# Attention and squared-ReLU FFN on one core: the last TensorE transposes of the steady loop go to DMA, the attention half behind them moves earlier, and one load moves behind a transpose

## The chip, the cores and the metric

The kernel runs on one core of one Trainium2 chip. The metric is device time in microseconds (us), the median of several executions. Only one execution of each run has a trace.

The engines are named as in the traces: TensorE (PE) does the matrix products, VectorE (DVE), ScalarE (ACT) and GpSimd (POOL) the element-wise work, and SyncE (SP) issues the transfers (DMA). PSUM is the on-chip memory that the products of this kernel are written to, in buffers called banks; SBUF is the on-chip memory of all its other tiles.

## The reference

```python
# q, k, v: (8, 8, 576, 64) float32; w_in: (512, 2048); w_out: (2048, 512)
scores = (q @ k.T) / sqrt(64)                      # per batch and head
mask = (rel >= 0) & (rel < 64)                     # causal window of 64
attn = softmax(where(mask, scores, -1e9)) @ v
x = attn.transpose(0, 2, 1, 3).reshape(4608, 512)
h = maximum(x @ w_in, 0)
out = (h * h) @ w_out                              # (4608, 512)
```

The 4608 tokens are nine blocks of 512. A block has four attention tiles of 128 tokens, two pairs.

## The kernel before

After a start of some 74 us, which brings the weights and works on the first blocks, the kernel is a loop of stages. A stage weaves four things by a position between 0 and 1: the down-projection of block g-1 (seven products in place of eight, in 14 steps), the up-projection of block g (16 groups of four matmuls), the attention of block g+1 and the loads for later ones. The events are sorted by position; that order is the program order of every engine.

```python
def attention(g):
    c = 4 * g
    ev = []
    dx = 0.34 if g == 3 else 0.275
    def sc(i):
        S_(i); expo(i)                     # TensorE scores, ScalarE exponential
        later(2, lambda: keep(i))          # VectorE mask, two ticks later
        tick()
    def to_xT(i):
        if g == 3:
            X(i)                           # four TensorE transposes
            copy_xT(i)                     # VectorE, out of PSUM
            tick()
        else:
            if i % 2:
                dma_xT(i // 2)             # one DMA transpose for a pair
    def va(i):
        V(i); norm(i); tick()              # TensorE values, VectorE normalisation
    for h in range(2):
        a, b, t = c + 2 * h, c + 2 * h + 1, 0.46 * h + (0.1 if g == 3 else 0.0)
        ev += [(t + 0.02, lambda a=a: sc(a)), (t + 0.021, lambda b=b: sc(b)),
               (t + 0.25, lambda a=a: va(a)), (t + 0.251, lambda b=b: va(b)),
               (t + dx, lambda a=a: to_xT(a)), (t + dx + 0.0001, lambda b=b: to_xT(b))]
    return ev

def UP(g, f):                              # one up-projection group
    hps = ps_up.tile([P, 512], FP32, name="hps", tag="ps_u")     # two buffers in PSUM
    ...                                    # four matmuls
    hrelu = hrp.tile(...)
    nc.scalar.activation(out=hrelu[:], in_=hps[:], func=AF.Relu)
    if f in SQ_ACT or g == 2 and f in (2, 9):
        ...                                # square on ScalarE, from hrelu
    else:                                  # square on VectorE, from hps and hrelu
        nc.vector.scalar_tensor_tensor(out=h2_of(g)[:, f, :], in0=hps[:], scalar=0.0,
                                       in1=hrelu[:], op0=ALU.max, op1=ALU.mult)
    tick()

def loads(p):
    for h in range(2):
        t, a = 0.46 * h, p + h
        ...                                # (t + 0.06) DMA transposes of k and q of pair a
            ev.append((t + (0.28 if a - 1 == TAILS[1] else 0.14), lambda a=a, x=kq: load(a + 1, x)))
            ev.append((t + 0.3, lambda a=a, x=kq: load(a + 1, "kqv"[len(x):])))
```

A load also carries the work that GpSimd does with it: casts to half precision and, for values, copies between two buffers. `S_` of tile i writes a PSUM bank that the normalisation of two tiles before has to free. SyncE issues all transfers in program order, so one that waits holds all behind it (run e7 below has the cost of such a place). `TAILS` names two pairs, 10 and 15, whose loads are arranged differently; `tick()` counts steps of the program, and `later(2, ...)` puts work two steps further down.

The softmax here doesn't subtract the row's maximum and nothing guards it: scores larger than these inputs give would overflow.

Of the kernel before, what the change touches and what calls it, by code (L numbers as in the profile page):

```python
# [40 lines left out]
def kernel(  # L41
# [16 lines left out]
    TAILS = (10, 15)  # L58
# [27 lines left out]
    def later(n, fn):  # L86
        if n == 0:
            fn()
        else:
            put_off.append([n, fn])  # L90

    def tick():
        for e in list(put_off):
            e[0] -= 1
            if e[0] <= 0:
                put_off.remove(e)
                e[1]()
# [65 lines left out]
    def fetch_tail(nm, p):  # L163

        src = {"k": k, "q": q, "v": v}[nm]
        for i in (2 * p, 2 * p + 1):
            if nm == "q":
                if i % 2 == 0:
                    st = two_tiles()
                sts[nm, i] = st[:, i % 2]  # L170
                for n in range(2):
                    fetch_rows(sts[nm, i], src, tail_seq(i) + n, S - 64, 64, 64 * n)
            else:
                st = sts[nm, i] = two_tiles()
                for n in range(2):
                    fetch_rows(st[:, n], src, tail_seq(i) + n, S - 128)
# [92 lines left out]
    def copy(eng, out, in_, scale=1.0):  # L269
        if eng is nc.scalar:  # L270
            nc.scalar.activation(out=out, in_=in_, func=AF.Copy, scale=scale)  # L271
        elif scale == 1.0:
            eng.tensor_copy(out=out, in_=in_)  # L273
        else:
            eng.tensor_scalar(out=out, in0=in_, scalar1=scale, scalar2=None, op0=ALU.mult)
# [19 lines left out]
    def cast_q(i, eng=nc.gpsimd):  # L295
        copy(eng, pair16(q16s, "q16", i // 2)[:, i % 2], sts["q", i])

    def cast_v(i, eng=nc.gpsimd):
        copy(eng, v_evs[i % NV][:, :, 0:D], sts["v", i])
# [15 lines left out]
    def xT_of(g):  # L315
        if g not in xTs:
            xTs[g] = xtp.tile([P, 4, DMC, P], FP16, name="xT", tag="xT")
        return xTs[g]
# [37 lines left out]
    def att_bank(name, dtype=FP32):  # L356
        return ps_att.tile([P, 2, 512], FP32, name=name, tag="ps_a")
# [59 lines left out]
    def S_(i):  # L417
        sc = att_bank("sc")
        scv = sc[:].rearrange("p a (h b t) -> p a h b t", h=HP, b=2)
        for a in range(2 if i < 4 else 0):  # L420
            nc.tensor.matmul(sc[:, a, :], ident[:], minus[i > 0], start=True, stop=False,
                             skip_group_check=True)
        for hp in range(HP):
            for blk in range(2):
                for hh in range(2):
                    r0 = 64 * hh
                    qT = q_cols(i)[r0:r0 + 64, hp, :]
                    qT = qT[:, 64 * blk:64 * blk + 64]
                    nc.tensor.matmul(scv[:, hh, hp, blk, :], keys(i, hp, r0, blk), qT,  # L429
                                     start=i >= 4, stop=True, skip_group_check=i < 4)  # L430
        scs[i] = sc
        pms[i] = attw.tile([P, 2, HP * 2 * 64], FP16, name="pm", tag="pm")

    def expo(i, part=slice(0, 2)):
        nc.scalar.activation(out=pms[i][:, part], in_=scs[i][:, part], func=AF.Exp,  # L435
                             scale=1.0 / float(D) ** 0.5)

    def keep(i, part=slice(0, 2)):
        mask = mask_first if is_first(i) else mask_inner
        nc.vector.tensor_tensor(  # L440
            out=pms[i][:, part], in0=pms[i][:, part],
            in1=mask[:].rearrange("p (o a) r -> p o (a r)", o=1)
            .to_broadcast([P, part.stop - part.start, 512]), op=ALU.min)

    def V(i):
        ps = att_bank("av")
        avs[i] = ps[:, :, 0:4 * 66].rearrange("p a (h e) -> p a h e", h=4)
        for h in range(H):
            for blk in range(2):
                vv = (v_ods if blk == 0 else v_evs)[i % NV]  # L450
                h0 = h // 2 * P + blk * 64
                nc.tensor.matmul(  # L452
                    avs[i][64 * blk:64 * blk + 64, h // 4, h % 4, 0:65],
                    pms[i][:, h % 2, h0:h0 + 64], vv[:, h, 0:65], start=True, stop=True)

    def norm(i):
        if i // 2 not in xs:
            xs[i // 2] = attw.tile([P, 2, 2, HP, D], FP16, name="x_sb", tag="x_sb", bufs=2)
        rden = smallp.tile([P, 2, 4, 1], FP32, name="rden", tag="rden")
        nc.vector.reciprocal(out=rden[:], in_=avs[i][:, :, :, 64:65])  # L460
        nc.vector.tensor_tensor(  # L461
            out=xs[i // 2][:, i % 2], in0=avs[i][:, :, :, 0:D],
            in1=rden[:].to_broadcast([P, 2, 4, D]), op=ALU.mult)

    def xT_cols(i):
        return xT_of(i // 4)[:, i % 4]

    def X(i):
        xps[i] = att_bank("xt_ps")[:, 0, :].bitcast(FP16)[:, 0:DMC * P].rearrange(
            "p (c t) -> p c t", c=DMC)  # L470
        for c in range(DMC):
            nc.tensor.transpose(out=xps[i][:, c, :],  # L472
                                in_=xs[i // 2][:, i % 2, c // 2, 2 * (c % 2):2 * (c % 2) + 2, :],
                                identity=ident[:])

    def copy_xT(i, eng=nc.vector):
        copy(eng, xT_cols(i), xps[i])

    def dma_xT(p):

        nc.sync.dma_start_transpose(
            out=xT_of(p // 2)[:, p % 2 * 2:p % 2 * 2 + 2].rearrange("p n c t -> p (n c) t"),
            in_=xs[p][:].rearrange("p n a h d -> p (n a h d)"))
# [234 lines left out]
    def attention(g):  # L718
        c = 4 * g
        ev = []  # L720
        dx = 0.34 if g == 3 else 0.275

        def sc(i):
            S_(i)
            expo(i)
            later(2, lambda: keep(i))
            tick()

        def to_xT(i):
            if g == 3:  # L730
                X(i)
                copy_xT(i)
                tick()
            else:
                if i % 2:
                    dma_xT(i // 2)

        def va(i):
            V(i)
            norm(i)  # L740
            tick()

        for h in range(2):
            a, b, t = c + 2 * h, c + 2 * h + 1, 0.46 * h + (0.1 if g == 3 else 0.0)
            ev += [(t + 0.02, lambda a=a: sc(a)), (t + 0.021, lambda b=b: sc(b)),
                   (t + 0.25, lambda a=a: va(a)), (t + 0.251, lambda b=b: va(b)),
                   (t + dx, lambda a=a: to_xT(a)), (t + dx + 0.0001, lambda b=b: to_xT(b))]
        return ev

    def load(p, part):  # L750

        if p in TAILS:
            for nm in part:
                fetch_tail(nm, p)
        else:
            for nm in part:
                fetch_two(nm, p)
        both = (2 * p, 2 * p + 1)
        if "k" in part:
            for i in both:  # L760
                if p in TAILS:
                    k16s["tail", i] = st16.tile([P, 2, H, D], FP16, name="k16", tag="k16")
                    nc.gpsimd.tensor_copy(out=k16s["tail", i][:], in_=sts["k", i][:])
                else:
                    cast_k(i)
        if "q" in part:
            for i in both:
                cast_q(i)
        if "v" in part:
            for i in both:  # L770
                if p in TAILS:
                    for n, vv in enumerate((v_ods, v_evs)):
                        nc.gpsimd.tensor_copy(out=vv[i % NV][:, :, 0:D], in_=sts["v", i][:, n])
                else:
                    cast_v(i)
                    shift_v(i)
# [6 lines that stand above are left out]
            if a < NCK // 2:  # L783
                ev.append((t + 0.06, lambda a=a: (dma_k(a), dma_q(a))))
                if a not in TAILS:
                    ev.append((t + 0.3, lambda a=a: halo_apart(a)))
            if a + 1 < NCK // 2:
                kq = "k" if a + 1 in TAILS else "kq"
                ev.append((t + (0.28 if a - 1 == TAILS[1] else 0.14), lambda a=a, x=kq: load(a + 1, x)))
                ev.append((t + 0.3, lambda a=a, x=kq: load(a + 1, "kqv"[len(x):])))  # L790
        return ev

# [3 lines left out]
    for g in range(2, NTB + 1):  # L796
# [3 lines left out]
        ev = even(out_seven(g - 1))  # L800
# [39 lines left out]
```

## Time and profile before

| | before |
|---|---|
| median of 3 (later of 6) | 293.33 us (292.78) |
| span of the profiled execution | 290.4 us |
| beginning of the loop (first down-projection group) | 74.19 us |
| that group to the next stage's: edited stage, then the two after it | 30.44, 28.92, 28.88 us |
| TensorE waits after 74 us, with a releaser | one, 0.2 us |

A stage between two such beginnings has 28.9 us of matmuls. The edited stage is longer by 1.5: 0.9 are transposes, and 0.57 are a score group, because its first half sits 0.1 later than elsewhere and the next stage's does not. So TensorE has no slack after 74 us: work taken from it should shorten the kernel.

### The profile page before, as it was taken

What the parts mean: (1) busy time and instruction counts of PE and PEld (TensorE: products, weight loads), DVE (VectorE), ACT (ScalarE), POOL (GpSimd) and SP (SyncE); (2) the same over time, 40 slices, a digit from 0 to 9 for tenths busy, and PEclk for the clock granted to TensorE, in tenths of its full rate; (3) what the DMA queues carried; (4) which work ended last, traced back from release to release, by engine and by line L of the source; (5) the groups of instructions that cost most, each with busy time, mean ns of one, the idle gap of its engine ahead of it and who ended that gap; (6) DMA issues with size and microseconds to landing.
All of it is one profiled execution on the core that took longest, in us unless ns stands there. A gap on an engine that the chain in (4) does not pass through costs nothing.

```text
span 290.4 us, 7514 instructions
## 1 busy us (share of the span) xinstructions
PE 284.5 (98%) x3062; PEld 197.3 (68%) x3062; DVE 212.6 (73%) x393; ACT 192.2 (66%) x304; POOL 114.7 (40%) x171
## 2 busy tenths in 40 slices
PE   7999999999999999999999999999999999999995
PEld 5768888755666766666666666666666666666684
DVE  3779998869967776766887687668767876554493
ACT  2789898959777576757575857485748575666500
POOL 3702967757337702525564735250537300000000
PEclk9999999999999999999999999999999999999999
DMA  7999999989999678999999989699969802300143
GB/s 216 342 392 302 287 288 297 367 217 233 168 218 178 142 211 183 219 184 279 202 223 216 275 191 213 136 279 213 250 112 278 150 2 64 119 0 2 72 109 109
DMA packets 151842, 57.64 MB, mean 198 GB/s; under 512 B 128256, under 2 KB 143616, under 8 KB 151808
## 3 DMA queue, kind: packets, MB, share of 16 engines
q1 hardware_dynamic: 151808, 57.16, 82.4%
q8 instruction: 24, 0.39, 0.6%
q14 instruction: 10, 0.08, 0.1%
HBM read 38.80 MB, written 9.44 MB: 166 GB/s over the span
## 4 chain that ended last, share of the span: by engine, by line
PE 88%; DVE 6%; ACT 2%; DMA 2%; SPq 2%; issue 0%; POOL 0%; POOLq 0%
PE hps L530 32%; PE opsC L616 10%; PE opsD L616 9%; PE hps L502 8%; PE opsA L616 8%; PE ops L576 5%; PE opsB L616 5%; PE av L452 4%; PE sc L429 3%; DMA v_st<-in_v_dram 2%; DVE hs_all L604 1%; PE xt_ps L472 1%; DVE pm L440 1%; SPq L130 1%; DVE x_sb L461 1%; ACT pm L435 1%
## 5 line engine op out<-in xcount | busy, mean ns | idle before, releaser
L530 PE MATMUL hps<-xT,w_in_sb 128*128 128x512 f16 x448 | 112.9, 379 | 0.2 <-DVE h L540 0.2
L534 ACT ACTIVATE hrelu<-hps 128x512 f32<-128x512 f32 x112 | 66.7, 597 | 63.7 <-PE hps L530 63.4
L616 PEld LDWEIGHTS <-h 128*128 128x128 f16 x624 | 60.5, 98 | 20.7 <-issue 0.2
L530 PEld LDWEIGHTS <-w_in_sb 128*128 128x128 f16 x448 | 42.4, 98 | 32.7 <-issue 0.4
L540 DVE SCALAR_TENSOR_TENSOR h<-hps,hrelu 128x512 f16<-128x512 f32 x54 | 37.2, 689 | 32.3 <-ACT hrelu L534 32.1
L273 POOL COPY v_od<-v_ev 64x512 f16<-64x512 f16 x54 | 38.2, 707 | 6.3 <-ACT v_ev L271 2.4
L537 ACT ACTIVATE h<-hrelu 128x512 f16<-128x512 f32 x58 | 36.5, 630 | 1.6
L435 ACT ACTIVATE pm<-sc 128x1024 f16<-128x1024 f32 (+1 forms) x40 | 35.4, 941 | 3.3 <-PE sc L429 3.3
L616 PE MATMUL opsA<-w_out_sb,h 128*128 128x256 f16 x240 | 31.0, 273 | 0.0
L616 PE MATMUL opsD<-wb_all,h 128*128 128x256 f16 x240 | 30.9, 273 | 0.0
L616 PEld LDWEIGHTS <-hs_all 128*128 128x128 f16 x256 | 25.0, 98 | 8.6
L502 PE MATMUL hps<-xT,w_in_sb 128*128 128x256 f16 x256 | 30.1, 273 | 0.0
L502 PEld LDWEIGHTS <-w_in_sb 128*128 128x128 f16 x256 | 24.2, 98 | 3.0
L273 POOL CAST k<-kq_st 128x512 f16<-128x512 f32 x17 | 11.9, 697 | 35.6 <-DMA kq_st<-in_k_dram 35.6
L461 DVE TENSOR_TENSOR x_sb<-av,rden 128x512 f16<-128x512 f32 x36 | 24.9, 692 | 1.2
L440 DVE TENSOR_TENSOR pm<-pm,mask_inner 128x1024 f16<-128x1024 f16 x25 | 20.2, 811 | 5.8 <-ACT pm L435 5.8
L273 POOL CAST q<-kq_st 128x512 f16<-128x512 f32 x22 | 14.5, 658 | 14.9 <-DMA kq_st<-in_q_dram 14.4
L638 DVE SCALAR_TENSOR_TENSOR osb_all<-opsD,u 128x512 f32<-128x512 f32 x14 | 9.7, 691 | 11.3 <-PE opsD L616 11.3
L273 POOL CAST v_ev<-kq_st 128x512 f16<-128x512 f32 x16 | 12.5, 778 | 11.3 <-DMA kq_st<-in_v_dram 10.8
L616 PE MATMUL opsC<-w_out_sb,h 128*128 128x256 f16 x128 | 16.4, 273 | 0.0
L616 PE MATMUL opsC<-w_out_sb,hs_all 128*128 128x256 f16 x128 | 16.4, 273 | 0.0
L616 PE MATMUL opsB<-wb_all,hs_all 128*128 128x256 f16 x128 | 16.4, 273 | 0.0
(104 smaller groups left out, 374.1 us busy)
## 6 DMA issues: line engine op xcount, KB each, us to landing
kq_st<-in_k_dram SPq DMA_DIRECT2D x26, 256.0 KB, 3.9
kq_st<-in_v_dram SPq DMA_DIRECT2D x24, 256.0 KB, 4.1
out_dram<-osb_all SPq DMA_DIRECT2D x12, 512.0 KB, 4.1
kq_st<-in_q_dram SPq DMA_DIRECT2D x18, 256.0 KB, 4.2
v_st<-in_v_dram SPq DMA_DIRECT2D x16, 256.0 KB, 5.2
k_st<-in_k_dram SPq DMA_DIRECT2D x7, 512.0 KB, 5.5
q_st<-in_q_dram SPq DMA_DIRECT2D x7, 512.0 KB, 5.6
out_dram<-osb_all SPq DMA_DIRECT2D x11, 256.0 KB, 2.4
```

Source lines behind the costliest of these rows:

```text
L273: eng.tensor_copy(out=out, in_=in_)
L435: nc.scalar.activation(out=pms[i][:, part], in_=scs[i][:, part], func=AF.Exp, scale=1.0 / float(D) ** 0.5)
L440: nc.vector.tensor_tensor(out=pms[i][:, part], in0=pms[i][:, part], in1=mask[:].rearrange("p (o a) r -> p o (a r)", o=1) .to_broadcast([P, ...
L452: nc.tensor.matmul(avs[i][64 * blk:64 * blk + 64, h // 4, h % 4, 0:65], pms[i][:, h % 2, h0:h0 + 64], vv[:, h, 0:65], start=True, stop=True)
L461: nc.vector.tensor_tensor(out=xs[i // 2][:, i % 2], in0=avs[i][:, :, :, 0:D], in1=rden[:].to_broadcast([P, 2, 4, D]), op=ALU.mult)
L502: nc.tensor.matmul(hps[:, f, :], w_in_sb[:, c, (2 * j + f) * P:(2 * j + f + 1) * P], xT_of(p // 2)[:, n0:n0 + 2, c, :], start=(c == 0), st ...
L530: nc.tensor.matmul(hps[:], w_in_sb[:, c, f * P:(f + 1) * P], xT_of(g)[:, :, c, :], start=(c == 0), stop=(c == DMC - 1))
L534: nc.scalar.activation(out=hrelu[:], in_=hps[:], func=AF.Relu)
L537: later(2 if f == 0 else 0, lambda: nc.scalar.activation(out=h2_of(g)[:, f, :], in_=hrelu[:], func=AF.Square))
L540: nc.vector.scalar_tensor_tensor(out=h2_of(g)[:, f, :], in0=hps[:], scalar=0.0, in1=hrelu[:], op0=ALU.max, op1=ALU.mult)
L576: nc.tensor.matmul(ops_of[ts][:], h2s[0][:, f, ts * P:(ts + 1) * P], w_out_sb[:, f, :], start=(f == 0), stop=(f == FFC - 1))
L616: nc.tensor.matmul(rows_of(bank, m), a[:, kk, m * P:(m + 1) * P], w[:, kk], start=(first and kk == 0 and (m == 0 or bank in apart)), stop= ...
```

## The change

The intent is to take the last 16 TensorE transposes out of the loop. Block 3's x goes through DMA like that of all later blocks. For the second pair to be there in time, the second half of that attention begins at 0.43 of the stage, a third of a stage behind the first, instead of 0.56. One stage on, the keys and queries behind the first tail pair are loaded after the transpose of x instead of ahead of it.

```diff
-        dx = 0.34 if g == 3 else 0.275
...
         def to_xT(i):
-            if g == 3:
-                X(i)
-                copy_xT(i)
-                tick()
-            else:
-                if i % 2:
-                    dma_xT(i // 2)
+            if i % 2:
+                dma_xT(i // 2)
...
-            a, b, t = c + 2 * h, c + 2 * h + 1, 0.46 * h + (0.1 if g == 3 else 0.0)
+            a, b = c + 2 * h, c + 2 * h + 1
+            t = (0.1, 0.43)[h] if g == 3 else 0.46 * h
...
-                   (t + dx, lambda a=a: to_xT(a)), (t + dx + 0.0001, lambda b=b: to_xT(b))]
+                   (t + 0.275, lambda a=a: to_xT(a)), (t + 0.2751, lambda b=b: to_xT(b))]
...
-  ev.append((t + (0.28 if a - 1 == TAILS[1] else 0.14), lambda a=a, x=kq: load(a + 1, x)))
+  ev.append((t + (0.28 if a in (TAILS[0], TAILS[1] + 1) else 0.14), lambda a=a, x=kq: load(a + 1, x)))
```

## The prediction

> **What bounds the kernel now.** I read the page's busy shares first, then the chain that ended last, then a table by stage, then the chain in order of time inside the stage that the change edits, and last the queue that issues the transfers.
>
> The page of the kernel before:
>
> ```profile
> span 290.4 us, 7514 instructions
> PE 284.5 (98%) x3062; PEld 197.3 (68%) x3062; DVE 212.6 (73%) x393; ACT 192.2 (66%) x304; POOL 114.7 (40%) x171
> PEclk9999999999999999999999999999999999999999
> PE 88%; DVE 6%; ACT 2%; DMA 2%; SPq 2%; issue 0%; POOL 0%; POOLq 0%
> ```
>
> TensorE is busy for 98% of the span at full granted clock, and 88% of the chain that ended last is TensorE. Busy alone would not settle it. The Trainium skill, "Perfetto Trace Analysis", opening note, calls matmul busy time a bad metric because matmuls are pipelined. So I ask instead whether each stage lasts as long as its list of matmuls at the pace at which they follow one another. From the second stage on, the kernel runs as a loop: each turn weaves 64 up-projection matmuls, 112 down-projection matmuls, the scores and value products of four attention tiles and the loads of later blocks. The table of stages (TensorE only; columns: window, its length, busy time with instructions, granted clock, DMA share, GB/s), from the first down-projection group to the next turn's scores, then two turns from scores to scores:
>
> ```profile
> 74.35:104.06 29.71, 29.71 (x322) 1.00 0.90 179
> 104.06:132.98 28.92, 28.92 (x306) 1.00 1.01 205
> 132.98:161.90 28.92, 28.92 (x309) 1.00 1.16 235
> ```
>
> The reader is to see that the latter two last the same 28.92 us and that none has an uncovered microsecond. The list explains the length. In the chain a group of four up-projection matmuls takes 0.86 us and a group of eight down-projection ones 0.87, so 16 x 0.86 + 14 x 0.87 = 25.9; two score groups at 0.57 and two value groups at about 0.64 with roughly 0.1 of set-up each add 2.8; 28.7 in all. Two more things agree: in the list of waits TensorE, from 74 us to the end, waits once for 0.2 us, and the first line of the three is longer by 0.8. That is the stage with the edit.
>
> The chain in that stage (start, length, what):
>
> ```profile
> 86.19 0.86 PE hps L530 x4
> 87.06 0.45 PE xt_ps L472 x8
> 87.50 0.87 PE opsC L616 x8
> ...
> 100.21 0.87 PE opsD L616 x8
> 101.08 0.45 PE xt_ps L472 x8
> 101.53 0.86 PE hps L530 x4
> ```
>
> Eight transposes of x stand between two matmul groups, twice, with no gap before or after. They are TensorE work on the path that sets the end, 0.45 us a time. All later blocks already turn x by DMA.
>
> **What the Trainium skill says.** "TensorE: Matmul & The Clock Gate", Part 4: PE-mode transpose, gives about 390 ns for a 128x128 bf16 transpose in isolation and about 275 ns in one kernel, and says that a DVE copy out of PSUM must follow. In this trace one record lasts 219 ns (median), but eight of them occupy 0.45 us of the chain, 56 ns each; the pace, not the record, is what can be won. From the page's 275 ns I would have estimated 4.4 us for 16, five times too much. The copy is there: two DVE copies of 0.42 us per pair. "Advanced Engine Details and Errata", X-Bar Transpose (TRN2), says that transpose DMAs are as fast as regular DMAs: here the ten transposes of x land a median 3.4 us after issue, the loads after 3.9 to 4.2, which agrees. "DMA: Bandwidth & Descriptors", Rules for kernel authors, says that a transpose beside ordinary DMAs needs nothing; transposes and loads already share the one queue here. So the new transposes only need a place in that queue.
>
> **The change, part by part.**
>
> First, block 3's x. It removes 16 transposes on TensorE, 2 x 0.45 = 0.90 us of the chain, and four DVE copies, 4 x 0.415 = 1.7 us, which are off the path. It adds two DMA transposes. Their queue time is about 1.25 us each when nothing holds them. The queue issues up to 95.8 us, then stands until the output stores at 100.6, which end up waiting 4.7 us for DVE. 2.5 us more fit into that hole, at the cost of the loads behind each x going out 1.2 to 3 us later. Value: -0.90 us.
>
> Second, the second half of block 3's attention moves from 0.56 to 0.43 of the stage, so its scores go from 91.0 to about 86.9, its value products from 97.7 to about 94.5. No work is added or removed. It exists to have x in time: the normalised x of the second pair should be done near 96.5 instead of 99.9, the transpose is then issued at about 96.5, and even with 5 us to land (the slowest group in this stretch, the key transposes, took up to 6.1) it is there at 101.5 to 102.6. The first up-projection of block 3 starts at about 104.6 (105.5 now, less 0.9). Slack 2 to 3 us. Value: 0.
>
> Third, in the next stage the keys and queries that follow the first tail pair are loaded at 0.74 instead of 0.60, behind the transpose of x. The queue of the kernel before in that place, and the reader of what it brings:
>
> ```profile
> 125.75 2.41 SPq L121 DMA_DIRECT2D kq_st<-in_k_dram  x2
> 128.20 1.89 SPq L121 DMA_DIRECT2D kq_st<-in_q_dram  x2
> 130.19 2.06 SPq L481 DMA_TRANSPOSE xT<-x_sb  x1
> 132.29 1.21 SPq L121 DMA_DIRECT2D kq_st<-in_v_dram  x2
> ...
> 134.43 1.03 PE L530 MATMUL hps<-xT,w_in_sb 128*128 128x512 f16 x4
> ```
>
> DVE finished this x at 126.9 (the last normalisation starts at 126.21 and takes 0.69), yet its transpose goes out at 130.19, behind four loads, and lands 4.1 us later, 134.3. The up-projection that reads it starts at 134.43. So it just makes it: about 0.1 us of slack, nothing to win there now. If TensorE came 0.9 us earlier to that point and the queue did not, TensorE would stand for up to 0.8 us and the first part's gain would be lost. With the third part x goes out near 126 to 127 and lands near 131, slack of 2 to 3 us. The displaced loads go out about 2 us later; their casts move from 130.3 to about 132 for the keys and up to 136 for the queries, while the transpose of these keys stands at 135.36 behind an output store. It should not be held. Value: 0 by itself; it lets the first part's 0.9 through.
>
> Sum: -0.90 us, everything behind it moves up by as much, because the later stages are lists of matmuls without gaps.
>
> **The rivals.**
>
> (a) The earlier scores make a new stop in the middle of the edited stage. For: DVE has no idle between 83.3 and 91.8, and the two masks of 0.69 each, in place of two copies of 0.74 together, now fall into it; ScalarE must put two exponentials of 0.96 between two relus, and the up-projection has two PSUM buffers, so a late square holds the matmuls two groups on. The score tiles also reuse the banks that the normalisation frees at 85.7 and 86.5, and the first wants its bank at about 86.9. I work out the square of the up-projection just behind the scores done at about 91.4 to 92.0, and its bank wanted at 91.8. Against: every later stage puts scores at the same place between groups without a stop. Cost 0 to 0.4 us: the total becomes -0.5.
>
> (b) The transfers become the bound: DMA is at 0.90 in this stage and 1.0 to 1.2 in the next two, and the new transposes delay values and tail keys. For: GpSimd waits mainly on transfers. Against: those waits are off the path, and stages with a DMA share of 1.16 run at the same 28.92. Only an x later than its matmuls would count; cost then 0 to 2 us, total +1 at worst.
>
> (c) More is won than the sum, as DVE gets 1.7 us back. For: nothing; TensorE has no wait on DVE of note. I give it no microseconds.
>
> **Range and chances.** The time before is 293.33 us, and its three runs span 1.3 us; 293.33 - 0.90 = 292.43. Rival (a) at a third chance would add some 0.1, but the fourth execution known, the profiled one with 292.34, says that the median of three sits a little high. I say 292.4. For the range I take the gain as 0.2 to 1.1 and the spread of a median of three as about 0.8: 291.2 to 293.8. Two per cent are 5.9 us: the removed work is a sixth of that, and slower by so much would need a wait on transfers in every stage. Faster 0.01, within 2% 0.97, slower 0.02.
>
> **What would show it.** Right: no transposes of x from TensorE after 74 us (48 left of 64); the stage from its first down-projection group to the next scores at 28.8 instead of 29.71; the following stages still 28.9; two new DMA transposes of x issued at about 86 and 96; in the next stage its x issued near 126 to 127, ahead of the loads. Step (a) shows as a TensorE wait on DVE or ScalarE between 86 and 93; step (b) as up-projections waiting on the DMA of x at the beginning of a stage. The prediction is wrong if a stage after the edit is no longer 28.9, or if the beginning or end, which the change does not touch, moves by more than the gain.

## The result, and the profile after

The changed kernel takes 293.15 us (median of 6, 292.79 to 293.92), the kernel before 292.78 us (median of 6). The ratio is 1.0016 with a 95% interval of 0.9995 to 1.0037; a ratio here is the mean of one kernel's fast runs over the mean of the other's of the same rounds, so not quite the ratio of the medians. That is "the same", inside the range, and yet the 0.9 us are not there.

The page of the changed kernel, its span and busy line:

```profile
span 291.0 us, 7486 instructions
PE 284.2 (98%) x3046; PEld 196.3 (67%) x3046; DVE 213.7 (73%) x389; ACT 192.2 (66%) x304; POOL 114.9 (39%) x171
```

Sixteen TensorE instructions fewer, four VectorE instructions fewer, and a span 0.6 us longer. The work left as planned; something else came. The table by stage (TensorE, same windows as the prediction's, moved to this trace's beginnings):

```profile
74.49:104.29 29.80, 29.02 (x305) 1.00 0.96 194
104.29:133.21 28.92, 28.92 (x305) 1.00 1.00 205
133.21:162.09 28.88, 28.88 (x305) 1.00 1.20 233
```

The edited stage is 29.80 us instead of 29.71, but only 29.02 of them are busy. The kernel before had no gap here; now 0.78 us of TensorE stand empty. The next two stages are as before. So the gain was made and given back inside the same stage. (Of the 0.6 us by which this span is longer, 0.5 come from elsewhere: in the two stages with small stops near 201 and 231 us, which take 29.21 and 28.77 us instead of 28.93 and 28.55. They are taken up further down.) The timeline of TensorE of the changed kernel shows where (start, length, engine, line, what; in brackets idle time and releaser):

```profile
90.37 1.03 PE L530 MATMUL hps<-xT,w_in_sb 128*128 128x512 f16 x4
91.23 1.04 PE L616 MATMUL opsD<-wb_all,h 128*128 128x256 f16 x8
93.05 1.89 PE L530 MATMUL hps<-xT,w_in_sb 128*128 128x512 f16 x8 [0.78 <-DVE h L540]
```

The group of eight that starts at 91.23 takes 0.87 us of pace, so the next could begin at 92.10. It begins at 93.05: a stop of 0.95 us. (The bracket says 0.78, because the record of the last matmul runs past the pace at which matmuls follow.) It waits for line 540, the square of the up-projection two groups before, which must leave the PSUM bank. The timeline of VectorE of the changed kernel just ahead:

```profile
87.94 0.68 DVE L638 SCALAR_TENSOR_TENSOR u<-opsB,p 128x512 f32<-128x512 f32 x1
89.49 0.88 DVE L440 TENSOR_TENSOR pm<-pm,mask_inner 128x1024 f16<-128x1024 f16 x1 [0.88 <-ACT pm L435]
90.29 1.09 DVE L604 TENSOR_TENSOR h<-h,hs_all 128x1024 f16<-128x1024 f16 x1
91.31 1.09 DVE L440 TENSOR_TENSOR pm<-pm,mask_inner 128x1024 f16<-128x1024 f16 x1
92.32 0.68 DVE L540 SCALAR_TENSOR_TENSOR h<-hps,hrelu 128x512 f16<-128x512 f32 x1
```

The square's relu was done at 90.86 (ScalarE, start 90.25, 0.61 long). The square itself starts at 92.32, because two masks (line 440) and a sum (line 604) stand ahead of it in the program. In the kernel before, the masks of these tiles came behind the crowded stretch (VectorE of the kernel before):

```profile
93.22 0.69 DVE L440 TENSOR_TENSOR pm<-pm,mask_inner 128x1024 f16<-128x1024 f16 x1 [1.42 <-ACT pm L435]
94.13 1.13 DVE L440 TENSOR_TENSOR pm<-pm,mask_inner 128x1024 f16<-128x1024 f16 x1 [0.22 <-ACT pm L435]
```

There is a second thing to see: in the changed kernel mask and sum take 0.88, 1.09 and 1.09 us. They take 0.68 to 0.69 in run e3 below, where GpSimd is silent. GpSimd of the changed kernel at that moment:

```profile
88.55 1.28 POOL L273 COPY v_od<-v_ev 64x512 f16<-64x512 f16 x2
89.89 0.95 POOL L273 CAST v_ev<-kq_st 128x512 f16<-128x512 f32 x1
90.91 1.97 POOL L273 COPY v_od<-v_ev 64x512 f16<-64x512 f16 x2
```

GpSimd works with hardly a pause. The Trainium skill, "SBUF — State Buffer", Who interferes with whom, says that a DVE instruction with two SBUF inputs contends with a GpSimd instruction that reads SBUF. Masks and sums have both inputs in SBUF, and they are stretched. The square has one input in PSUM and keeps its 0.68. The trace agrees with the page so far; the experiment e3 tests it. Two more readings support it. The two engines end their instructions by turns: mask 90.37, cast 90.84, sum 91.38, first copy 91.86, mask 92.40, second copy 92.87; each VectorE end comes 0.54 us after GpSimd's, each GpSimd end 0.47 after VectorE's, as if one worked while the other waited. And over all 13 traces after 74 us, the 615 masks and sums with no GpSimd work beside them took 0.67 to 0.69 us, those with some beside them up to 1.55, while squares took 0.67 to 0.69 in both cases. The transfers do not explain it: from 89.4 to 92.3 us the DMA share is 1.23 in the changed kernel and still 1.10 in e3.

### The profile page after: what moved, and what is told of

Same layout as the page of the kernel before. It is cut to its first block, busy times and chain, and to the rows that moved or that the text cites. A ratio compares the mean times of both kernels' runs of the same rounds, so it can differ in the third digit from the quotient of the medians.

```text
span 291.0 us, 7486 instructions
## 1 busy us (share of the span) xinstructions
PE 284.2 (98%) x3046; PEld 196.3 (67%) x3046; DVE 213.7 (73%) x389; ACT 192.2 (66%) x304; POOL 114.9 (39%) x171
## 4 chain that ended last, share of the span: by engine, by line
PE 60%; DVE 6%; ACT 1%; issue 0%
PE hps L530 28%; PE opsC L616 9%; PE opsD L616 9%; PE opsA L616 6%; PE opsB L616 4%; DVE hs_all L604 3%; PE av L452 2%; PE sc L429 2%; DVE pm L440 1%; DVE h L540 1%; DVE x_sb L461 1%; ACT pm L435 1%; PE opsD L674 1%; PE opsE L616 1%; ACT hrelu L534 0%
## 5 line engine op out<-in xcount | busy, mean ns | idle before, releaser
L273 POOL CAST k<-kq_st 128x512 f16<-128x512 f32 x17 | 11.0, 649 | 37.5 <-DMA kq_st<-in_k_dram 37.5
```

The costliest lines, as they stand in the source:

```text
L273: eng.tensor_copy(out=out, in_=in_)
```

## The experiments

Theory A: the earlier scores (part two) put two masks into a full stretch of VectorE, GpSimd stretches them, the PSUM bank comes free late, and TensorE stops for as long as the removed transposes took. Theory B: the DMA transposes load the transfers and cost what the matmuls gave.

The loop begins at different times in different executions, 74.2 to 76.8 us in the 13 profiles, although the program ahead of it is the same. So a common measure was taken that leaves the start out: from the second of the two down-projection groups ahead of the scores (85.16 us before, 85.34 after) to the first one of the next stage (104.63, 104.86). I call it the stretch.

| run | stretch, us | stops after 74 us | median, us | ratio to before (95%) |
|---|---|---|---|---|
| before | 19.47 | 230.0: 0.18 | 292.78 | 1 |
| changed | 19.52 | 92: 0.95 (0.78); 201: 0.17; 231: 0.38 | 293.15 | 1.0016 (0.9995 to 1.0037) |
| changed, again (e5) | 19.72 | 93: 1.14 (0.97); 202: 0.33 | 292.74 | 0.9971 (0.9930 to 1.0012) |
| scores alone (e1) | 19.97 | 93: 0.50 (0.34) | 294.12 | 1.0025 (0.9995 to 1.0055) |
| x by DMA alone (e2) | 18.58 | 229: 0.18 | 291.35 | 0.9938 (0.9910 to 0.9967) |
| the same, again (e9) | 18.58 | 203: 0.32 | 292.38 | 0.9967 (0.9940 to 0.9994) |
| values later (e3) | 18.59 | 230: 0.18 | 293.02 | 0.9995 (0.9962 to 1.0029) |
| square on ScalarE (e4) | 18.58 | 230: 0.18 | 293.08 | 0.9991 (0.9954 to 1.0029) |

The stops at 92 and 93 us are by pace, with the timeline's bracket beside them; the others are brackets. The kernel before was timed anew in each series (medians 293.05, 293.27 and 293.23 us of eleven; 292.78 of six is the first series), so a ratio tells more than a difference between two rows.

### e1: the scores alone

```diff
-  t = 0.46 * h + (0.1 if g == 3 else 0.0)
+  t = (0.1, 0.43)[h] if g == 3 else 0.46 * h
+  if g == 3:
+      dx = (0.5, 0.34)[h]        # TensorE transposes stay, the first pair's behind the scores
```

> The kernel before with the second part alone: the second half of block 3's attention at 0.43 of the stage, x still turned by 16 TensorE transposes (the first pair's are put behind the scores, so that they take no score bank from them). Theory A (the earlier scores put two masks into a stretch of VectorE that is full and slowed by GpSimd, and the up-projection's PSUM bank comes free late): TensorE stops once for 0.7 to 1.0 us in this stage and the time is 0.7 to 1.0 us above before, near 293.7. Theory B (the DMA transposes themselves, through the load on the transfers, cost what the removed matmuls gave): no stop, the same time as before within 0.3 us.

The stretch is 19.97 us, 0.50 longer than before, with a stop of 0.50 (by pace) at the same place behind the same square. That is less than the 0.7 to 1.0 expected, and the trace shows why: the first pair's eight transposes, 0.45 us of TensorE work, happened to fall between the scores and the stop and filled that much of the wait. 0.50 + 0.45 is the stop of the changed kernel. The masks and sum were stretched in the same way (0.88, 1.10, 1.09). Part two costs the stop without any DMA transpose; theory B does not explain it.

### e2: x by DMA with the scores where they were

```diff
-  t = (0.1, 0.43)[h] if g == 3 else 0.46 * h
+  t = (0.1, 0.56)[h] if g == 3 else 0.46 * h
+  dx = 0.255 if g == 3 and h else 0.275      # ahead of the output store at 0.821
```

> The changed kernel with the second half of the attention left at 0.56, its DMA transpose put ahead of the output store; the load order as changed. Theory A: no scores in the full stretch, so no stop, 0.8 to 0.9 us below before, near 292.0. Theory B: the transfers are all there, so the time stays that of before within 0.3 us. If x of the second pair lands late (issue near 99.5, landing 3 to 5 us later, wanted at 104.6), a stop of under 0.5 us stands at the beginning of the next stage instead.

The stretch is 18.58 us, shorter than before by 0.89, which is the 16 transposes. TensorE busy fills the edited stage whole:

```profile
74.47:103.29 28.82, 28.82 (x307) 1.00 1.00 181
```

Its DMA share is 1.00 against 0.90 before, so the transfers are fuller and TensorE does not feel it. Theory B falls. The time is 0.62% below before, more than 0.89 us can be (0.3%); what the rest is, the one trace does not tell, and the repeat (e9) did not bring it again.

### e3: GpSimd kept quiet

```diff
-  ev.append((t + 0.3, ... load(a + 1, "v")))
+  ev.append((t + (0.585 if a == 7 else 0.3), ... load(a + 1, "v")))
```

> The changed kernel with the value load, the casts and the copies of pair 8 moved from 0.30 to 0.585 of the stage, so that GpSimd does next to nothing between 87.5 and 94 us. Theory A with GpSimd as the cause of the slow masks and sums: the three VectorE instructions between 89.5 and 92.3 follow each other at about 0.61 us instead of 0.80, 1.02 and 1.01, the stop shrinks from 0.95 to 0.2 us or less, and the time is 0.7 to 0.9 us below the changed kernel. Rival A2 (the order on VectorE and ScalarE alone makes the stop, whatever GpSimd does): the stop stays above 0.6 us.

The timeline of VectorE with the values later:

```profile
89.91 0.69 DVE L440 TENSOR_TENSOR pm<-pm,mask_inner 128x1024 f16<-128x1024 f16 x1 [0.86 <-ACT pm L435]
90.52 0.68 DVE L604 TENSOR_TENSOR h<-h,hs_all 128x1024 f16<-128x1024 f16 x1
91.12 0.69 DVE L440 TENSOR_TENSOR pm<-pm,mask_inner 128x1024 f16<-128x1024 f16 x1
91.72 0.69 DVE L540 SCALAR_TENSOR_TENSOR h<-hps,hrelu 128x512 f16<-128x512 f32 x1
```

and GpSimd in the same stretch:

```profile
85.02 1.69 POOL L273 CAST q<-kq_st 128x512 f16<-128x512 f32 x2 [0.27 <-DMA kq_st<-in_q_dram]
95.61 0.61 POOL L273 CAST v_ev<-kq_st 128x512 f16<-128x512 f32 x1 [8.89 <-DMA kq_st<-in_v_dram]
```

The order on VectorE is the same; only GpSimd is silent. The three instructions ahead of the square follow at 0.61, 0.60 and 0.60 us instead of 0.80, 1.02 and 1.01: 1.02 us less, and the stop of 0.95 is gone. The stretch is 18.59, the full gain. So the order alone does not make the stop (rival A2 falls); order and GpSimd together do. The timed runs do not show it: they scatter from 292.05 to 293.88, and the ratio is 0.9995. The expected 0.7 to 0.9 us below the changed kernel was met in the trace and missed in the times. The traced execution was the fastest of the six; whether the stop was absent in the slower ones, no trace shows. Nor does any explain why e2, with the same stretch and timed in the same series, is 1.7 us lower in its median.

### e4: the square off VectorE

```diff
-  if f in SQ_ACT or g == 2 and f in (2, 9):
+  if f in SQ_ACT or g == 2 and f in (2, 7, 9):
```

> The changed kernel with one square (up-projection 7 of block 2) on ScalarE instead of VectorE. Theory A: the bank comes free about 91.5 instead of 93.0, before TensorE wants it at 92.1, so the stop goes and the time is 0.8 to 0.95 us below the changed kernel, 0.5 to 0.8 below before. Theory B: no change within 0.3 us. If another bank then comes late, a stop of under 0.4 us is seen one or two groups on.

VectorE is as slow as in the changed kernel (0.88, 1.09, 1.09), but the square no longer stands behind it: ScalarE starts it at 91.43 and takes 0.63. No stop, stretch 18.58. This is a second sign, by another edit, that the bank held by that square is what TensorE waited for (ScalarE and TensorE of e4; the second line has no bracket):

```profile
91.43 0.63 ACT L537 ACTIVATE h<-hrelu 128x512 f16<-128x512 f32 x1
...
92.65 1.89 PE L530 MATMUL hps<-xT,w_in_sb 128*128 128x512 f16 x8
```

The times again scatter (291.54 to 294.81) and show nothing.

### e5: the changed kernel again

> The changed kernel once more, unaltered, on the same chip as the next three. The stop near 92 us belongs to the order of the work, so it should be there again at 0.8 to 1.0 us, and from the second of the two down-projection groups ahead of the scores to the next stage's first one there should again be 19.5 us. The further stops of the first profile near 201 us and 230 us (0.3 to 0.5 each) are open: if they are the change's, they come again; if they hang on when GpSimd happens to run, they can differ by 0.2 us or more. Time within 0.4% of before.

The stop is there again, 1.14 by pace (0.97 by the timeline's bracket), a little more than the 0.8 to 1.0 expected, and the stretch is 19.72 instead of 19.5: here the first mask takes 1.08 us instead of 0.88. The small further stop near 202 us is there again too, the one near 231 us is not. Its ratio to before is 0.9971 where the first series gave 1.0016: the same kernel, half a per cent apart in two series. That is the measure of what a ratio can carry here.

### e6, e10, e11: the third part taken back

```diff
-  0.28 if a in (TAILS[0], TAILS[1] + 1) else 0.14
+  0.28 if a == TAILS[1] + 1 else 0.14         # on top of e2
```

> Part one with the scores left at 0.56 (the run that won 0.9 us in the trace), but with the third part taken back: the keys and queries after the first tail pair loaded at 0.60 again, ahead of x. If the third part is needed, x of that stage goes out near 129.3 to 130 and lands near 133.4 to 134.2 while it is wanted at 133.66: a stop of 0 to 0.6 us at the beginning of the stage, time 0 to 0.6 us above the same kernel with the third part. Rival: the queue moves up with everything else and there is no stop; then the third part is worth nothing.

In the first look x went out at 131.35, landed 4.0 us later and was wanted at 136.14: no stop (292.5 us, ratio 0.9960). But in this execution the loop began at 76.79 us, 2.5 us later than in e2, while x went out only 1.2 us later than in the kernel before, whose loop began at 74.19. So it was looked at twice more.

> The version of e9 with the third part taken back, a second look. In the first look there was no stop, but TensorE was 2.5 us late from the first 74 us while the queue was not, so x had that much more time. If this look begins its loop near 74.3 us, x should land about 134 to 135 and be wanted at 133.66, a stop of 0.3 to 1 us; if it begins near 76 us there should again be none. Rival: no stop in either case, as the queue moves with TensorE.

> The same kernel as the run before it, a third look, for the same question: a stop of 0.3 to 1 us at the first up-projection of block 4 if the loop begins near 74.3 us, none if it begins near 76 us.

These began at 75.03 and 74.89, and both (single runs, state unknown) stopped at the first up-projection of block 4 for 0.6 us by the bracket. The stage that holds it is 29.68 and 29.67 us long instead of 28.88: 0.80 us lost (single times 292.46 and 292.97). The chain in order of time of the second look (start, length, what):

```profile
129.52 0.87 PE opsD L616 x8
130.39 0.30 PE hps L530 x2
130.69 4.43 DMA xT<-x_sb
135.12 0.05 issue
135.17 1.04 PE hps L530 x4
```

The transfer itself is now a link of the chain. So the third part is worth 0.8 us, but only to a kernel whose TensorE comes early. In the changed kernel the stop at 92 us had put TensorE back to its old time. Its queue did profit (x out at 127.17 instead of 130.19), and by these times nothing needed it; the changed kernel without the third part was not run.

### e7: x where the formula puts it, behind the store

```diff
-  t = (0.1, 0.43)[h] if g == 3 else 0.46 * h
+  t = (0.1, 0.56)[h] if g == 3 else 0.46 * h      # dx stays 0.275
```

> Part one with the scores left at 0.56 and the transpose of the second pair where the formula puts it, 0.835 of the stage, which is behind the output store that waits for VectorE. Theory: x goes out at 101.5 to 102.5 instead of 99.6, lands 3 to 4.5 us later at 104.5 to 107, and is wanted at 104.74, so TensorE stops for 0.3 to 2 us at the first up-projections of block 3 and the gain of 0.9 is mostly or wholly lost. This would be what the second part was made to avoid. Rival: it lands in time, no stop, 0.9 us below before; then the second part had no purpose.

The queue of this run:

```profile
100.34 0.38 SPq L653 DMA_DIRECT2D out_dram<-osb_all  x1
100.77 2.00 SPq L481 DMA_TRANSPOSE xT<-x_sb  x1
```

x lands 4.5 us after issue, at 105.3, and the first up-projection of block 3 starts at 105.34 after a wait of 0.35 on it. The next stage is 29.45 us instead of 28.92. So 0.53 of the 0.89 us are lost (292.38 us, ratio 0.9962, interval 0.9917 to 1.0006). The issue was earlier than I had said, and the loss sits at the low end of what was expected. This is what the second part was made to avoid. It avoids it by moving the scores; e2 does it by moving one issue ahead of the store. That way is tighter: in the six traces with it, x landed 0.05 to 1.2 us before it was wanted (e9 the least), in the changed kernel 4.3 us before.

### e8: the same cure in two later stages

```diff
+  or g in (6, 7) and f == 3       # square on ScalarE, on top of e2
```

> Part one with the scores left at 0.56, the third part kept, and the square of up-projection 3 of blocks 6 and 7 on ScalarE: the same cure as in the edited stage, in the two later stages where the same kind of stop was seen. The stage from 219 to 248 us should be 28.30 instead of 28.55 and the one before it 28.87 to 28.88; time 0.25 us below the same kernel without it, near 291.1. If ScalarE is then late with another relu, a stop of that size appears one group on and nothing is won.

There was no stop at 201 or 230 us. The last stage with attention, expected at 28.30, measured 28.42, and two others were 0.1 and 0.26 longer, in an execution at a granted clock of 0.999. The median is 292.1 us, ratio 0.9953 (0.9910 to 0.9995). As four executions without the cure (e1, e6, e10, e11) had 28.21 to 28.25 in that stage, I take it as inconclusive.

### e9: x by DMA alone, again

> The version with part one, the scores left at 0.56 and x ahead of the store, once more and unaltered, on the same chip as the next two. If its 0.6% below before was a real gain of 0.9 us plus luck with the first 74 us (which the change does not touch and which took 74.2 to 76.8 us in the profiles so far), its trace again shows 18.58 us from the second of the two down-projection groups ahead of the scores to the next stage's first one, no stop in that stage, and the times come out 0.2 to 0.5% below before.

The stretch is 18.58 again, with a loop that began at 76.53 us this time. The median is 292.38, ratio 0.9967 (0.9940 to 0.9994). The two series of this kernel, 0.9938 and 0.9967, have intervals wholly below 1, as has e8, which contains it. The gain that the traces show is about 0.9 us, 0.3%. That the larger figure of the first series was luck with the start is not shown: its trace began its loop at 74.31 us, that of the kernel before at 74.19. This version is below the kernel before in both of its series, though by far less than 2%; the changed kernel is not, its intervals hold 1 in both. It was not timed in one series with the changed kernel (e8, which contains it, was: 292.10 against 292.74 us in e5, with intervals that overlap); the traces put it 0.9 to 1.1 us ahead in the stretch.

## Why the prediction was right or wrong

**The range and the class were right.** 293.15 us lies in 291.2 to 293.8, and the result is within 2%. The named 292.4 and the gain of 0.9 behind it did not come: the measured difference is +0.4 us in the medians of the first series and -0.5 in the second, with no gain that can be told from zero.

**The value of the first part was right.** 16 transposes were to be worth 0.90 us. Where nothing stops TensorE, six kernels (e2, e3, e4, e6, e7, e8) show a stretch shorter by 0.88 or 0.89.

**The step that failed is rival (a), "Cost 0 to 0.4 us: the total becomes -0.5".** The mechanism is the one described: masks in the full stretch, the square late, the bank two groups on. The size was wrong. The prediction worked out "the square of the up-projection just behind the scores done at about 91.4 to 92.0, and its bank wanted at 91.8". The bank was wanted at 92.1, and the square was done at 93.0: the stop was 0.95 us, not 0 to 0.4. The mis-sized term is the time of the three VectorE instructions ahead of the square. The prediction gave a mask 0.69, and at the undisturbed pace of 0.61 from start to start (e3) the three take 1.8 us; they took 0.80, 1.02 and 1.01, together 2.83, because GpSimd was at work in SBUF at the same time. The difference of 1.0 is, within 0.1, the stop. The trace before had the warning: the second mask of these tiles took 1.13 us at 94.13, while the first took 0.69 at 93.22. Of GpSimd the prediction asked only whether its own waits count ("those waits are off the path"), not what it does to VectorE.

**The counter-argument to (a) failed with it.** "Every later stage puts scores at the same place between groups without a stop" compared only the place in the stage, and the kernel before already has a stop of 0.18 us at 230. Later stages do have masks and sums of 1.09 us beside GpSimd (changed kernel, 195.26 and 196.27, 224.69 and 225.71) and stop for 0.17 and 0.38 us. Why they lose so much less than the edited stage was not worked out.

**The second part was given the value 0.** It costs the stop, 0.95 us, and its purpose can be had without it (e2 against e7), with less slack. The prediction had x of the second pair issued at about 96.5; it went out at 98.24, when the stop had delayed its values, and was in time all the same.

**The third part was right.** "TensorE would stand for up to 0.8 us" without it: 0.80 in two looks out of three. That it "lets the first part's 0.9 through" could not show in the changed kernel, where the 0.9 was gone already.

**Rival (b), the transfers,** was rightly set aside: DMA shares of 0.96 to 1.20 and no wait on x in the changed kernel. Rival (c) was worth nothing, as said.

One of the prediction's own signs of being wrong came up: a stage after the edit is no longer 28.9 us, but 29.21. The further stops of the changed kernel near 201 and 231 us (0.17 and 0.38 us) look like the same kind: TensorE waits for a square, and masks and sums beside GpSimd's casts and copies are stretched in the microseconds before. They also occur in the kernel before (0.18 at 230 us) and in e9 (0.32 at 203 us). Whether the change makes them more likely is open.

## What to carry to other kernels

Before moving work to an earlier slot, list what every engine does in that slot, those off the critical path too: an instruction of 0.69 us took 1.09 because a neighbour off the critical path was at work in the same memory. If a result is late, look first whether its own issue can go ahead of a waiting one in the queue, before moving the work that produces it. And when a gain is less than the scatter of the start, measure it in a stretch of the trace that begins after the start.

## What the Trainium skill lacked or had wrong

- "TensorE: Matmul & The Clock Gate", Part 4: the 390 and 275 ns of a PE transpose are durations of one. In a row of eight they cost 0.45 us, 56 ns each, and removing 16 shortened the stretch by 0.89 us. The part gives no figure for the pace; Part 1 of the page has 56 ns for matmuls of this width in a row, and nothing there says that transposes keep it.
- "SBUF — State Buffer", Who interferes with whom: that a DVE instruction with two SBUF inputs contends with GpSimd is right and explained the result. No size is given for this pair. Here masks and sums went from a pace of 0.61 to 1.01 us, and a GpSimd cast or copy from 0.61 to 0.95. The page's summary says that the second to issue blocks fully, and the trace agrees: the ends come by turns, 0.54 and 0.47 us apart, 1.01 for one of each. That is less than the sum of the two durations alone (0.68 + 0.61), so these do not give the size. Which engine waits depends on who is first: the sum at 84.35 us of the changed kernel took 0.68, and the cast that began at 84.37 took 1.14.
- "Advanced Engine Details and Errata", X-Bar Transpose (TRN2): as fast as a regular DMA holds, but what counted was the place in the queue. Transposes of x landed 2.7 to 5.6 us after issue, and one issue behind a store cost 0.53 us.
- No page that I read has it: how far the start of a kernel that brings its weights scatters. The same first part took 74.2 to 76.8 us in 13 profiles.
